# A routed expert kernel: first slot's products in float32, and token numbers with the one-hot as moving operand

## The chip, the cores and the metric

One core of a Trainium2 chip runs one kernel. The metric is the device time of one launch in microseconds (us), from the first to the last thing the core does. The engines are TensorE (PE, with PEld for its weight loads), VectorE (DVE), ScalarE (ACT), GpSimd (POOL) and SyncE (SP), which here only issues transfers. Each engine works through its own queue in order; semaphores hold an instruction until what it reads is there.

## What is computed

The reference has three stages. Attention with a memory term (4 batches, 8 heads, 576 positions, 64 wide) gives 2304 rows of 512. A router then assigns rows to 8 experts by a global greedy rule, 288 rows each, and expert e gives `relu(x[mask] @ w1[e]) @ w2[e]` (512 to 1024 to 512). Last, one dense layer for all rows: `h = x @ w_in`, `g = h * clip(h + 3, 0, 6) / 6`, `out = g @ w_out` (512 to 2048 to 512).

```python
for idx in order:                       # argsort(-logits.flatten())
    tok, e = int(idx) // E, int(idx) % E
    if assigned[tok] >= 0 or counts[e] >= cap:
        continue
    assigned[tok] = e
    counts[e] += 1
...
h = np.maximum(x[mask] @ w1[e], 0.0)
out[mask] = h @ w2[e]
```

All data are float32, and the assignment is discrete, so a product has to keep nearly all of float32's accuracy.

## The kernel before, in words

Attention fills the first 300 us and writes the rows to DRAM (`x_dram`). While it runs, `Convert` (L951) rounds part of w_in and w_out and puts them into DRAM as `wb`. Then `experts` (L1013) works in eight slots. A slot is one expert with its 288 tokens and has 24 chunks: 8 of the first kind (w1, w2 of that expert, 128 hidden units each) and 16 of the second (w_in, w_out). The list `order` (L1216) names them as (slot, kind, f), and one loop (L1261) goes through it.

A chunk has a first layer, `l1` (L1182), an evaluation `ev` (relu, or the clipped product), and a second layer, `l2` (L1212), which adds into four PSUM tiles `acc`. The second layer runs LAG = 2 chunks behind the first (`second`, L1231, with the list `pend`). Between the kinds `y_in` (L1173) copies the four sums to SBUF as the next kind's input; after the second kind `out_units` (L1143) transposes and scatters the result by token number.

Accuracy comes from splitting: a float32 value is written as hi + lo in float32r, and a product is three float32r products (hi with hi, hi with lo, lo with hi), so 12 for `l1` and 12 for `l2` of a chunk. For weights `split_w` (L1092) does it: ScalarE copies the raw tile to hi (L1106), GpSimd subtracts to get lo (L1108); in slot 0 the first six and then every sixth of these go to VectorE. `ahead` (L1221) calls it some chunks before their use. For the second kind the splits of odd chunks stay in SBUF (`WB`), those of even chunks go to DRAM (`hl`, L1112) and are loaded again in later slots (L1102). So slot 0 alone splits w_in and w_out. For activations the evaluation writes gh on ScalarE and gl on VectorE (L1201, L1208), and `x_in` and `y_in` do the same for x and y.

Raw weights come in through a ring of RAW = 4 tiles of 128x1024 (`load`, L1066), on SP's queue. The load of chunk f + 4 is issued when `split_w` has taken the second half of chunk f. In slot 0 the loads reach over both kinds; the last w_in/w_out pieces are rounded there (`Convert.rest`, L1004).

The router (`Router`, L515) finds each slot's expert and tokens while the slot before runs: `phase` (L804) searches two thresholds in four steps each on VectorE and ScalarE (L714, L716), `ids_units` (L916) turns positions into token numbers, and `gather` (L1056) fetches the rows with three indirect transfers on GpSimd's queue. For slot 0 nothing runs beside it. For the numbers, `oc` is a one-hot tile [128, 96, 20] (bfloat16), where `oc[:, :, j]` has a stride of 20 elements, and `ua` holds each token's number as 64 u + v, three times cumulated. The 20 products (L939, recorded on L701) have `oc[:, :, j]` as stationary and 6 columns of `ua` as moving operand; VectorE then copies, subtracts neighbours and joins u and v (L942 to L946).

The order on each engine's queue is set by a scheduler that simulates the program when it is built: it goes by program order and by its own estimate of when an instruction is ready. `step` (L1256) hands out the router's units at a rate per chunk, 1.4 in slot 0 and 0.9 later, and `mm` (L699) ties each router product behind the last product of the slot. On the chip the queues are then fixed: a TensorE product of the router whose input is late stops the slot's products behind it.

Of the kernel before, what the change touches and what calls it, by code (L numbers as in the profile page):

```python
# [514 lines left out]
class Router:  # L515
# [17 lines left out]
    def consts(self):  # L533
# [89 lines left out]
        sv = t("sv", [96, 4, 2])  # L623
        nc.vector.memset(sv, 0.0)
# [291 lines left out]
    def ids_units(self, pos, done):  # L916
# [96 lines left out]
def experts(ctx, tc, rt, x_dram, cv, w1, w2, out, ident, cap, B, S):  # L1013
# [7 lines left out]
    EVERY, FIRST = 6, 6  # L1021
# [44 lines left out]
    def load(s, j):  # L1066

        if j >= FA + FB * (s == 0):
            return
        if j >= FA:  # L1070
            f = j - FA
            raw = raws[s, 1, f] = wp.tile([128, 1024], F32, name="raw", tag="raw", bufs=RAW)
            if f < cv.pre // 2:
                nc.sync.dma_start(raw, cv.wb[:, f])
            else:
                conv.extend([lambda u=u: cv.rest(raw[:, u * 512:(u + 1) * 512], 2 * f + u) for u in range(2)])
            return
        f = j
# [3 lines left out]
        raw = wp.tile([128, 1024], F32, name="raw", tag="raw", bufs=RAW)  # L1082
        nc.sync.dma_start(raw[:, :512].rearrange("p (k n) -> p k n", k=KC),
                          w1[bass.ds(e, 1), :, f * 128:(f + 1) * 128].rearrange("o (k p) n -> p (o k) n", p=128))
        nc.sync.dma_start(raw[:, 512:], w2[bass.ds(e, 1), f * 128:(f + 1) * 128, :].rearrange("o p n -> p (o n)"))
        raws[s, 0, f] = raw
# [3 lines left out]
    cnt = [0]  # L1090

    def split_w(i, part):  # L1092
# [6 lines left out]
        W[i, part] = hi, lo  # L1099
# [16 lines left out]
    def mm3(p, lhs, rhs, first, last):  # L1116
        (ah, al), (bh, bl) = lhs, rhs
        nc.tensor.matmul(p, ah, bh, start=first, stop=False)  # L1118
        nc.tensor.matmul(p, ah, bl, start=False, stop=False)  # L1119
        rt.behind = nc.tensor.matmul(p, al, bh, start=False, stop=last)  # L1120

# [3 lines left out]
    def x_in(s):  # L1125

        XT[s] = []
        for c in range(KC):
# [6 lines left out]
            t = p[:, :cap]  # L1135
            if s:
                t = act.tile([128, cap], F32, name="t", tag="t", bufs=2)
                nc.scalar.activation(t, p[:, :cap], AF.Copy)
            rt.xin = nc.scalar.activation(hl[0], p[:, :cap], AF.Copy)
# [33 lines left out]
    def y_in(acc):  # L1173
        y = []
        for o, p in enumerate(acc):
            hl = parts("y", f"y{o}", 1)
# [3 lines left out]
        return y  # L1180

# [37 lines left out]
    nw = [0, 0]  # L1219

    def ahead(i):  # L1221

        for part in range(2):
            while nw[part] < min(i + 2 * SPLIT[0], len(order)):
                held = [j for j in range(i - part * LAG, nw[part] + 1) if j >= 0 and not (order[j][1] and order[j][2] % 2)]
                if len(held) > SPLIT[part] or order[nw[part]][0] not in reg or order[nw[part]][:1] + (0, 0) not in raws:
# [4 lines left out]
    def second():  # L1231
# [5 lines left out]
        l2(acc[s, kind], g, W.pop((i, 1)), f == 0, f == n - 1)  # L1237
        if f == n - 1:
            a = acc.pop((s, kind))
            if kind == 0:  # L1240
                X[s, 1] = y_in(a)
# [6 lines left out]
    for f in range(RAW):  # L1248
        load(0, f)
# [11 lines left out]
    for i, (s, kind, f) in enumerate(order):  # L1261
        step()
        if (kind, f) == (1, NEXT[s > 0]) and s + 1 < E:
            routed(s + 1)
            for u in range(RAW):
                load(s + 1, u)
# [12 lines left out]
        e = l1(kind, f, X[s, 1] if kind else XT[s], W.pop((i, 0)), rt.behind if kind and f == 1 else None)  # L1279
# [3 lines left out]
        pend.append((i, e()))  # L1283
        if (kind, f) in STORE and todo:
# [81 lines left out]
```

## Time and profile before

| | us |
|---|---|
| median of 3 runs | 1131.04 (1130.54 to 1137.7) |
| profiled execution, its own time | 1130.45 |
| its span, first to last instruction | 1128.6 |
| TensorE busy | 961.0 |
| VectorE busy | 727.9 |
| ScalarE busy | 605.6 |
| GpSimd busy | 435.8 |
[...]

Busy time is the union of an engine's instructions. Products on TensorE overlap in its pipeline, so the duration of one is longer than its share of the time: what counts is the distance between starts. Line numbers are those of the kernel before; router products all carry line L701. "idle before" in a row names what ended the idle time.

### The profile page before, as it was taken

The page shows a single profiled execution, that of the slowest core. Times are in us where ns is not written, and L with a number is a line of the kernel's source. Part 1 is how long each engine was busy: PE and PEld are TensorE (multiplying, and loading weights), DVE is VectorE, ACT ScalarE, POOL GpSimd, SP SyncE. Part 2 cuts the span into 40 slices and gives each one's busy share as a digit, 9 for nine tenths or more (in the row PEclk, how much of TensorE's full clock was granted, in tenths as well). Part 3 has the DMA queues.
Part 4 walks back from the last instruction along what each step waited for, and adds up shares of the span by engine and source line. Part 5 has one row for each costly group of instructions (what it writes and reads, how often), then busy time and mean ns, then how long its engine had stood idle before and what let it go on. Part 6 is the DMA issues. An engine that isn't in the chain of part 4 may idle for free.

```text
span 1128.6 us, 20123 instructions
## 1 busy us (share of the span) xinstructions
PE 961.0 (85%) x6748; PEld 885.6 (78%) x6748; DVE 727.9 (64%) x1933; ACT 605.6 (54%) x1499; POOL 435.8 (39%) x346
## 2 busy tenths in 40 slices
PE   4888888898317788789889889899989999999997
PEld 3676766675217688779789788889978999999996
DVE  7888897986773996783973856586385534234332
ACT  5786776875334764534653563455256235445442
POOL 7657556661424664331250044026104402603400
PEclk9999999998657997889999999899899899999999
DMA  7889879887133865349229525823752562572540
GB/s 172 240 239 258 232 205 266 206 228 202 43 99 112 297 214 163 96 146 270 84 73 286 138 75 195 222 82 119 232 148 68 183 202 90 182 243 73 181 159 21
DMA packets 122999, 190.28 MB, mean 169 GB/s; under 512 B 21904, under 2 KB 72464, under 8 KB 122896
## 3 DMA queue, kind: packets, MB, share of 16 engines
q1 hardware_dynamic: 119136, 179.54, 53.2%
q0 software_dynamic: 3072, 9.44, 2.8%
q8 instruction: 54, 0.88, 0.3%
q14 instruction: 49, 0.40, 0.1%
q10 hardware_dynamic: 688, 0.02, 0.0%
HBM read 144.60 MB, written 25.61 MB: 151 GB/s over the span
## 4 chain that ended last, share of the span: by engine, by line
PE 34%; DVE 20%; issue 8%; DMA 5%; ACT 1%; POOL 1%; POOLq 0%; DVEq 0%; ACTq 0%; SPq 0%
DVE rcmp L714 5%; PE h L1187 5%; PE acc L1119 5%; PE h L1188 5%; PE acc L1120 5%; PE h L1190 5%; PE acc L1118 5%; DMA rHw<-kd 4%; PE rp L701 2%; DVE gl L1201 2%; DVE gl L1208 2%; DVE cnt L717 1%; DVE t L1206 1%; DVE fl L725 1%; POOL w L1108 1%
## 5 line engine op out<-in xcount | busy, mean ns | idle before, releaser
L1108 POOL TENSOR_TENSOR w<-raw,w 128x512 fp32r<-128x512 f32 x135 | 180.6, 1352 | 383.5 <-ACT w L1106 291.4
L1119 PE MATMUL acc<-gl,w 128*128 128x288 f32 x512 | 156.7, 312 | 19.3 <-DVE gl L1208 13.0
L1120 PE MATMUL acc<-gh,w 128*128 128x288 f32 x512 | 153.4, 306 | 0.0
L1118 PE MATMUL acc<-gh,w 128*128 128x288 f32 x512 | 139.9, 310 | 13.7 <-ACT gh L1207 13.5
L1206 DVE SCALAR_TENSOR_TENSOR t<-t,pc 128x288 f32<-128x288 f32 x128 | 61.4, 480 | 117.4 <-ACT pc L1205 117.2
L1119 PEld LDWEIGHTS acc<-gl,w 128*128 128x128 f32 x512 | 101.8, 199 | 24.3 <-DVE gl L1208 16.7
L1204 ACT ACTIVATE t<-h,rthree 128x288 f32<-128x288 f32 x128 | 63.5, 496 | 102.8 <-PE h L1190 97.5
L1118 PEld LDWEIGHTS acc<-gh,w 128*128 128x128 f32 x512 | 93.9, 197 | 16.3 <-ACT gh L1207 16.2
L1106 ACT ACTIVATE w<-raw 128x512 fp32r<-128x512 f32 x144 | 89.6, 633 | 28.5 <-PE acc L1120 16.3
L282 ACT ACTIVATE P<-P,mx 128x128 f32<-128x128 f32 (+2 forms) x144 | 83.6, 581 | 37.1 <-DVE mx L267 35.7
L1120 PEld LDWEIGHTS acc<-gh,w 128*128 128x128 f32 x512 | 101.8, 199 | 0.0
L1201 DVE TENSOR_TENSOR gl<-t,gh 128x288 fp32r<-128x288 f32 x64 | 52.7, 824 | 73.6 <-ACT gh L1200 73.6
L1207 ACT ACTIVATE gh<-t 128x288 fp32r<-128x288 f32 x128 | 56.6, 444 | 64.4 <-DVE t L1206 64.4
L1208 DVE SCALAR_TENSOR_TENSOR gl<-t,gh 128x288 fp32r<-128x288 f32 x128 | 66.1, 517 | 29.8 <-ACT gh L1207 28.0
L1187 PE MATMUL h<-yh,w 128*128 128x288 f32 x256 | 74.4, 309 | 6.6 <-ACT pc L1205 6.6
L1119 PE MATMUL acc<-gl,WB 128*128 128x288 f32 x256 | 75.9, 303 | 2.7 <-DVE gl L1208 2.6
L246 PE MATMUL sc<-kh,qs 128*128 128x128 f32 (+3 forms) x128 | 49.7, 399 | 30.9 <-DVE qs L218 12.2
L1187 PE MATMUL h<-xh,w 128*128 128x288 f32 x256 | 75.3, 313 | 0.3 <-ACT gh L1200 0.3
L1120 PE MATMUL acc<-gh,WB 128*128 128x288 f32 x256 | 74.8, 298 | 0.0
L1188 PE MATMUL h<-xh,w 128*128 128x288 f32 x256 | 74.4, 310 | 0.0
L1188 PE MATMUL h<-yh,w 128*128 128x288 f32 x256 | 72.5, 301 | 0.0
L1187 PE MATMUL h<-yh,WB 128*128 128x288 f32 x256 | 71.1, 298 | 0.0
(294 smaller groups left out, 2806.8 us busy)
## 6 DMA issues: line engine op xcount, KB each, us to landing
w<-hl SPq DMA_DIRECT2D x112, 512.0 KB, 5.0
raw<-in_moe_w_dram SPq DMA_DIRECT2D x128, 256.0 KB, 4.3
kh<-knh SPq DMA_DIRECT2D x60, 144.0 KB, 2.6
raw<-in_moe_w_in_dram SPq DMA_DIRECT2D x16, 512.0 KB, 4.0
raw<-in_moe_w_out_dram SPq DMA_DIRECT2D x16, 512.0 KB, 4.6
hl<-w SPq DMA_DIRECT2D x16, 512.0 KB, 6.2
wb<-wf SPq DMA_DIRECT2D x28, 256.0 KB, 2.9
raw<-wb SPq DMA_DIRECT2D x14, 512.0 KB, 5.0
```

Source lines behind the costliest of these rows:

```text
L282: nc.scalar.activation(x[:, :w], x[:, :w], AF.Exp, bias=mx, scale=-1.0, accum_out=col)
L1106: nc.scalar.activation(hi, src, AF.Copy)
L1108: j = (nc.vector if v else nc.gpsimd).tensor_tensor(lo, src, hi.bitcast(F32), op=OP.subtract)
L1118: nc.tensor.matmul(p, ah, bh, start=first, stop=False)
L1119: nc.tensor.matmul(p, ah, bl, start=False, stop=False)
L1120: rt.behind = nc.tensor.matmul(p, al, bh, start=False, stop=last)
L1187: nc.tensor.matmul(p, wk[k][0], x[k][0], start=(k == 0), stop=False)
L1188: nc.tensor.matmul(p, wk[k][1], x[k][0], start=False, stop=False)
L1201: nc.vector.tensor_tensor(gl, t, gh.bitcast(F32), op=OP.subtract)
L1204: nc.scalar.activation(t, p, AF.Relu, bias=rt.three)
L1206: nc.vector.scalar_tensor_tensor(t, t, 6.0, pc, op0=OP.min, op1=OP.mult)
L1208: nc.vector.scalar_tensor_tensor(gl, t, 1.0 / 6.0, gh.bitcast(F32), op0=OP.mult, op1=OP.subtract)
```

## The change

Slot 0 uses float32 products on unsplit weights and activations: `l1_whole` for the first layer (4 products), one product for each of the four sums in `l2`, plain copies in `x_in` and `y_in` (odd ones on VectorE, even ones on ScalarE), one tile g instead of gh and gl. `ahead` starts with slot 1. The weights of the second kind are still split in slot 0, for later slots, but after the chunk's first layer and evaluation, and always on ScalarE and GpSimd. The ring has two tiles of 128x512 a chunk instead of one of 128x1024, and `load(i + RAW)` comes at the end of chunk i in slot 0; the first loads of slot 1 come out of the same sequence instead of with the expert's number. In the router, `ua` becomes the stationary operand and `oc[:, :, j]` the moving one; the result [6, 96] is copied to bfloat16 and turned by one product with a constant [6, 3] that subtracts neighbours and joins 64 u + v. Ten small VectorE instructions build that constant at the start.

```diff
@@ consts
-        sv = t("sv", [96, 4, 2])
-        nc.vector.memset(sv, 0.0)
+        dg = t("dg", [128, 3], BF)
+        nc.vector.tensor_scalar(ti[:, :1], pi, 1, None, op0=OP.logical_shift_right)
+        nc.vector.tensor_copy(bf, ti[:, :1])
+        nc.vector.tensor_scalar(ti[:, :1], pi, 1, None, op0=OP.bitwise_and)
+        nc.vector.tensor_copy(ef, ti[:, :1])
+        nc.vector.tensor_scalar(ef, ef, -63.0, 64.0, op0=OP.mult, op1=OP.add)
+        nc.vector.tensor_scalar(kb[:, 0:3], col[:, 0:3], bf, ef, op0=OP.is_equal, op1=OP.mult)
+        nc.vector.tensor_scalar(bf, bf, -1.0, None, op0=OP.add)
+        nc.vector.tensor_scalar(q2, col[:, 0:2], bf, ef, op0=OP.is_equal, op1=OP.mult)
+        nc.vector.tensor_tensor(kb[:, 0:2], kb[:, 0:2], q2, op=OP.subtract)
+        nc.vector.tensor_copy(dg, kb[:, 0:3])
@@ ids_units
-                self.mm(p[:96, :6], self.oc[:, :, j], st["ua"][:, j].rearrange("p a u -> p (a u)"),
+                self.mm(p[:6, :96], st["ua"][:, j].rearrange("p a u -> p (a u)"), self.oc[:, :, j],
                         start=(j == 0), stop=(j == NJ - 1))
-            sv = self.sv
-            nc.vector.tensor_copy(sv[:, :3], p[:96, :6].rearrange("p (a u) -> p a u", u=2))
-            d = wk.tile([96, 3, 2], F32, name="d", bufs=1)
-            nc.vector.tensor_tensor(d, sv[:, :3], sv[:, 1:], op=OP.subtract)
+            sv = wk.tile([6, 96], BF, name="sv", bufs=1)
+            nc.vector.tensor_copy(sv, p[:6, :96])
+            p = self.ps.tile([128, 512], F32, name="rp", tag="r", bufs=2)
+            self.mm(p[:96, :3], sv, self.dg[:6], start=True, stop=True)
             ids = wk.tile([96, 3], I32, name="ids", bufs=2)
-            self.last = nc.vector.scalar_tensor_tensor(ids, d[:, :, 0], 64.0, d[:, :, 1], op0=OP.mult, op1=OP.add)
+            self.last = nc.vector.tensor_copy(ids, p[:96, :3])
@@ load
-    def load(s, j):
+    def load(j):
+        s, kind, f = order[j]
+        if s and kind:
             return
...
+        raw = raws[j] = [wp.tile([128, 512], F32, name=f"raw{u}", tag=f"raw{u}", bufs=RAW) for u in range(2)]
+        if kind:
+            for u in range(2):
+                if f < cv.pre // 2:
+                    nc.sync.dma_start(raw[u], cv.wb[:, f, u * 512:(u + 1) * 512])
+                else:
+                    conv.append(lambda u=u: cv.rest(raw[u], 2 * f + u))
             return
...
@@ split_w
-        src = raws[s, kind, f][:, part * 512:(part + 1) * 512]
-        cnt[0] += 1
+        src = raws[i][part]
         nc.scalar.activation(hi, src, AF.Copy)
-        v = s == 0 and (cnt[0] % EVERY == 0 or cnt[0] <= FIRST)
-        j = (nc.vector if v else nc.gpsimd).tensor_tensor(lo, src, hi.bitcast(F32), op=OP.subtract)
-        if s == 0 and kind == 0:
-            after(tc, j, rt.last if v else rt.fetch)
+        nc.gpsimd.tensor_tensor(lo, src, hi.bitcast(F32), op=OP.subtract)
         if kind and f % 2 == 0:
             nc.sync.dma_start(hl[f // 2, part], w.bitcast(F32))
-        if part:
-            load(s, f + kind * FA + RAW)
+        if part and s and f + RAW < FA:
+            load(i + RAW)
@@ x_in (y_in alike)
+            if s == 0:
+                x = whole("x", f"x{c}", 1)
+                if c % 2:
+                    nc.vector.tensor_copy(x, p[:, :cap])
+                else:
+                    nc.scalar.activation(x, p[:, :cap], AF.Copy)
+                XT[s].append(x)
+                continue
@@ new
+    def l1_whole(kind, f, x, w, prev=None):
+        p = ps.tile([128, 512], F32, name="h", tag="h", bufs=2)[:, :cap]
+        for k in range(KC):
+            rt.behind = nc.tensor.matmul(p, w[:, k * 128:(k + 1) * 128], x[k], start=(k == 0), stop=(k == KC - 1))
...
+        def ev():
+            g = whole("g", "g", LAG + 2)
+            if kind == 0:
+                nc.scalar.activation(g, p, AF.Relu)
+            else:
...
+                nc.scalar.activation(t, p, AF.Relu, bias=rt.three)
+                nc.scalar.activation(pc, p, AF.Copy, scale=1.0 / 6.0)
+                nc.vector.scalar_tensor_tensor(g, t, 6.0, pc, op0=OP.min, op1=OP.mult)
+            return g
+        return ev
@@ l2
+            if not isinstance(g, tuple):
+                rt.behind = nc.tensor.matmul(p[:, :cap], w[:, o * 128:(o + 1) * 128], g, start=first, stop=last)
+                continue
@@ ahead
-    nw = [0, 0]
+    nw = [FA + FB] * 2
@@ main loop
-            for u in range(RAW):
-                load(s + 1, u)
+            for u in range(RAW if s else 0):
+                load(pos[s + 1, 0, u])
...
         pend.append((i, e()))
+        if s == 0:
+            for u in range(2 * kind):
+                split_w(i, u)
+            load(i + RAW)
```

## Rows read from the trace of the kernel before

**Rows 1.** First line of the page
```profile
span 1128.6 us, 20123 instructions
```

**Rows 2.** Stretches: length; busy (count) of PE, PEld, DVE, ACT, POOL; clock; DMA share, GB/s
```profile
346.70:466.20 119.50, 97.78 (x630) 91.75 (x630) 92.17 (x191) 72.37 (x163) 63.03 (x47) 0.87 0.59 192
466.20:567.80 101.60, 91.32 (x635) 87.13 (x633) 75.90 (x204) 52.76 (x126) 28.96 (x22) 0.95 0.46 145
959.30:1038.60 79.30, 78.94 (x602) 78.68 (x601) 28.22 (x53) 39.16 (x97) 26.92 (x22) 1.00 0.53 174
346.70:350.00 3.30, 3.30 (x14) 3.30 (x15) 2.67 (x7) 0.85 (x3) 0.00 (x0) 0.52 0.00 0
```

**Rows 3.** Waits of TensorE in slot 0: us in total, times, longest
```profile
PE acc L1118 <- ACT gh L1207: 6.2, 3, 4.3
PE acc L1119 <- DVE gl L1208: 5.1, 5, 1.9
PE rp L701 <- DVE roc L933: 3.8, 1, 3.8
```

**Rows 4.** Groups by line, VectorE, slot 0
```profile
L1208 DVE SCALAR_TENSOR_TENSOR gl<-t,gh 128x288 fp32r<-128x288 f32 x15 | 8.8, 589 | 1.0 <-ACT gh L1207 1.0
L1201 DVE TENSOR_TENSOR gl<-t,gh 128x288 fp32r<-128x288 f32 x8 | 6.5, 808 | 9.1 <-ACT gh L1200 9.1
```

**Rows 5.** Timeline of TensorE, attention: start us, us, then the merged instructions
```profile
127.65 1.84 PE L328 MATMUL av<-PT,vn 128*64 128x320 f32 x12
128.24 0.44 PE L328 MATMUL av<-PT,vn 128*64 128x320 f32 x2
128.51 0.71 PE L328 MATMUL av<-PT,vn 128*64 128x320 f32 x4
```

**Rows 6.** The same view, slot 6's first kind
```profile
959.30:987.60 28.30, 28.30 (x218) 28.28 (x217) 8.18 (x15) 13.60 (x33) 16.96 (x14) 1.00 0.56 182
```

**Rows 7.** Router's products (L701) by stretch (PE, PEld), one group, a hand-over
```profile
327.90:331.40 3.50, 3.46 (x20) 3.46 (x20) 0.50 0.88 284
892.45:895.80 3.35, 3.31 (x20) 3.35 (x20) 1.00 0.92 319
L701 PE MATMUL rw<-rXT,rR 128*128 128x512 bf16 (+1 forms) x16 | 3.5, 292 | 0.0
325.54 0.16 DVE L895 TENSOR_SCALAR ex<-rp 128x2 f32<-128x2 f32 x1 [0.31 <-PE rp L701]
```

**Rows 8.** Around slot 0's gather: timelines of POOL, DVE, SP; landing
```profile
332.41 4.95 POOL L1061 DMA_INDIRECT xg<-x_dram,ids  x1 [23.49 <-DVE rleft L914]
338.89 0.92 POOL L1061 DMA_INDIRECT xg<-x_dram,ids  x1 [0.30 <-issue]
333.84 2.48 DVE L1108 TENSOR_TENSOR w<-raw,w 128x512 fp32r<-128x512 f32 x4
335.24 0.38 SPq L1083 DMA_DIRECT2D raw<-in_moe_w_dram  x1
xg<-x_dram,ids POOLq DMA_INDIRECT x3, 6.8
xg<-x_dram,ids POOLq DMA_INDIRECT x3, 5.1
```

**Rows 9.** SP's timeline; transfers of slot 0 with landing; splits on the page
```profile
420.98 0.55 SPq L1083 DMA_DIRECT2D raw<-in_moe_w_dram  x1
raw<-wb SPq DMA_DIRECT2D x14, 512.0 KB, 5.0
raw<-in_moe_w_dram SPq DMA_DIRECT2D x16, 256.0 KB, 9.5
L1106 ACT ACTIVATE w<-raw 128x512 fp32r<-128x512 f32 x144 | 89.6, 633 | 28.5 <-PE acc L1120 16.3
L1108 POOL TENSOR_TENSOR w<-raw,w 128x512 fp32r<-128x512 f32 x135 | 180.6, 1352 | 383.5 <-ACT w L1106 291.4
```

**Rows 10.** Timeline of TensorE, its first product
```profile
12.02 0.48 PE L246 MATMUL sc<-kh,qs 128*128 128x128 f32 x1 [12.02 <-DVE qs L218]
```

More of the change, by code (lines that the diff above doesn't have):

```diff
@@ L1081, in load @@
         e = reg[s]
-        raw = wp.tile([128, 1024], F32, name="raw", tag="raw", bufs=RAW)
-        nc.sync.dma_start(raw[:, :512].rearrange("p (k n) -> p k n", k=KC),
+        nc.sync.dma_start(raw[0].rearrange("p (k n) -> p k n", k=KC),
                           w1[bass.ds(e, 1), :, f * 128:(f + 1) * 128].rearrange("o (k p) n -> p (o k) n", p=128))
-        nc.sync.dma_start(raw[:, 512:], w2[bass.ds(e, 1), f * 128:(f + 1) * 128, :].rearrange("o p n -> p (o n)"))
-        raws[s, 0, f] = raw
+        nc.sync.dma_start(raw[1], w2[bass.ds(e, 1), f * 128:(f + 1) * 128, :].rearrange("o p n -> p (o n)"))
     W = {}
     conv = []
-    cnt = [0]
     def split_w(i, part):
@@ L1098, in split_w @@
         hi, lo = w[:, :512], w[:, 512:]
-        W[i, part] = hi, lo
+        if s:
+            W[i, part] = hi, lo
         if kind and s:
@@ L1120, in mm3, with whole @@
         rt.behind = nc.tensor.matmul(p, al, bh, start=False, stop=last)
+    def whole(name, tag, bufs):
+        return act.tile([128, cap], F32, name=name, tag=tag + "h", bufs=bufs)
     def parts(name, tag, bufs):
@@ L1133, in x_in @@
                 nc.tensor.transpose(p[:, a * G:(a + 1) * G], XG[s][a][:, c * 128:(c + 1) * 128], ident[:G, :G])
-            hl = parts("x", f"x{c}", 1)
[L1135 to L1139, printed above, removed]
+            if s == 0:
[6 more added lines that the diff above has]
+                continue
+            hl = parts("x", f"x{c}", 1)
+            t = act.tile([128, cap], F32, name="t", tag="t", bufs=2)
+            nc.scalar.activation(t, p[:, :cap], AF.Copy)
+            nc.scalar.activation(hl[0], p[:, :cap], AF.Copy)
             nc.vector.tensor_tensor(hl[1], t, hl[0].bitcast(F32), op=OP.subtract)
@@ L1180, in y_in @@
         return y
+    def l1_whole(kind, f, x, w, prev=None):
+        p = ps.tile([128, 512], F32, name="h", tag="h", bufs=2)[:, :cap]
+        for k in range(KC):
+            rt.behind = nc.tensor.matmul(p, w[:, k * 128:(k + 1) * 128], x[k], start=(k == 0), stop=(k == KC - 1))
+            if prev is not None:
+                after(tc, rt.behind, prev)
+                prev = None
+        def ev():
+            g = whole("g", "g", LAG + 2)
+            if kind == 0:
+                nc.scalar.activation(g, p, AF.Relu)
+            else:
+                t = act.tile([128, cap], F32, name="t", tag="t", bufs=2)
+                pc = act.tile([128, cap], F32, name="pc", tag="pc", bufs=2)
+                nc.scalar.activation(t, p, AF.Relu, bias=rt.three)
[3 more added lines that the diff above has]
+        return ev
     def l1(kind, f, x, w, prev=None):
@@ L1224, in ahead @@
             while nw[part] < min(i + 2 * SPLIT[0], len(order)):
-                held = [j for j in range(i - part * LAG, nw[part] + 1) if j >= 0 and not (order[j][1] and order[j][2] % 2)]
-                if len(held) > SPLIT[part] or order[nw[part]][0] not in reg or order[nw[part]][:1] + (0, 0) not in raws:
+                held = [j for j in range(max(i - part * LAG, FA + FB), nw[part] + 1)
+                        if not (order[j][1] and order[j][2] % 2)]
+                if len(held) > SPLIT[part] or nw[part] not in raws and not order[nw[part]][1]:
                     break
@@ L1236, in second @@
             acc[s, kind] = [ps.tile([128, 512], F32, name=f"acc{o}", tag=f"acc{o}") for o in range(KC)]
-        l2(acc[s, kind], g, W.pop((i, 1)), f == 0, f == n - 1)
+        l2(acc[s, kind], g, W.pop((i, 1)) if s else raws[i][1], f == 0, f == n - 1)
         if f == n - 1:
@@ L1240, in second @@
             if kind == 0:
-                X[s, 1] = y_in(a)
+                X[s, 1] = y_in(s, a)
             else:
@@ L1248, in experts @@
     for f in range(RAW):
-        load(0, f)
+        load(f)
     for i in range(2):
@@ L1278, in experts @@
             conv.pop(0)()
-        e = l1(kind, f, X[s, 1] if kind else XT[s], W.pop((i, 0)), rt.behind if kind and f == 1 else None)
+        e = (l1 if s else l1_whole)(kind, f, X[s, 1] if kind else XT[s], W.pop((i, 0)) if s else raws[i][0],
+                                    rt.behind if kind and f == 1 else None)
         step()
```

17 lines of the change are left out of this document (6 added, 11 removed).

## The prediction, made before the result was known

> **What bounds the kernel now.** I read the span first, then busy time by stretch, then the waits of TensorE in the one stretch that the change rewrites. The profiled execution spans 1128.6 us [rows 1]; its own time is 1130.45, so 1.85 lies around the span, and it stands 0.6 below the median of the three runs (1131.04). All sums below are made against 1130.45. The eight slots begin at 346.7 us. Slot 0 takes 119.5 us to slot 1's first product, slot 1 101.6, and slot 6 79.3 with TensorE busy for 78.9 at a granted clock of 1.00 [rows 2]. So late slots are bound by TensorE alone, and slot 0 loses 40 us. [...] The waits name what it starves on: the two halves of g (6.2 + 5.1 us) and the one-hot positions (3.8 us) [rows 3]; all six waits of that list come to 21.7 us. The g halves cost VectorE 8.8 + 6.5 us, at 589 and 808 ns each [rows 4], and each chunk has to wait for its own.
>
> **Part 1, float32 products in slot 0.** Removed before the products: all splits of w1 and w2 (16 halves), the hi/lo work on x, y and g. The 32 splits of w_in and w_out stay, but come after the chunk's products and nobody in slot 0 waits for them. Each group of three float32r products becomes one float32 product: per chunk 8 in place of 24. The price of one: in attention six float32 products of 320 columns (three blocks, two heads) leave 12 records, so two records each [rows 5]. Records of the two heads run side by side (the pair at 128.24 takes 0.44 us together), and the next pair starts at 128.51: a step of 0.27 us; over all six pairs it is (1.84 - 0.44) / 5 = 0.28. That is 0.84 ns a column and record, so 288 columns cost 0.243 us a record, 0.486 a product. A float32r product goes by at 28.3 us / 218 = 0.130 us [rows 6], weight load included, so 128-column loads fit under 0.243. A chunk is then 8 x 0.486 = 3.89 us in place of 24 x 0.130 = 3.12. TensorE alone gets slower by 0.77 x 24 = 18 us over the slot; what is bought is the idle time.
>
> Slot 0's stretch holds 24 first and 22 second layers (two are late, beside slot 1): 46 x 4 x 0.486 = 89.4 us. To it: the start at the lower clock, 3.3 us at 0.52 [rows 2], which loses 1.6; the router's and transposes' work on TensorE, 3.5 + 3.5 us in rows [rows 7] and some 1.5 of small ones, 8.5; and waits that stay, 5 us (the one-hot 3.8 as now, 1 where y is copied). The g waits go: two chunks of lag are now 7.8 us, against the 0.6 us of the one VectorE step that an evaluation keeps, and what is queued before it. Sum 104.5, gain 15.0. Bounds: 19 with no wait left; 8 if the router's in-order stops grow to the 10 to 12 us that fit slot 1 (101.6 - 79.3 less its router work). The two late second layers cost 2 x (1.94 - 1.56) = 0.7 in slot 1.
>
> **Start of slot 0.** Now the gather is slow: its first issue holds GpSimd 4.95 us against 0.92 for the third, while VectorE runs four more weight splits of 0.68 us (2.48 together), and from 335.24 on three more chunks are loaded (split early, they freed the ring), in front of the last gathered rows, which take 6.8 us to land; slot 1's take 5.1 [rows 8]. After the change those VectorE splits are gone, and the ring lets chunk 4 load only after the first product, so both obstacles go. Landing: 332.4 + two issues of 1.2 (0.92 and the step between) + 5.1 gives 340 in place of 338.9 + 6.8 = 345.7; if the 4.95 is a first issue's own cost, 338.9 + 5.1 = 344. Gain 2 to 6; I take 4.5, nearer to the first, as the splits beside the slow issue are what differs, less a little for the transposes, which then come in one lot.
> [...]
>
> **Start of slot 1: what is late next.** Slot 1's first chunks are now loaded from 421 us on [rows 9], 45 us ahead. After the change they pass through the same ring of four: the second half of chunk i is freed by products two chunks on, and SP's queue is in order, so the next chunk's first half, the intermediate stores and the router's transfers all stand behind it. The lead is two chunks, 7.8 us in slot 0, about 7.0 at the seam. Inside slot 0 it needs 0.8 for two issues and 5.0 to land: it holds. At the seam a split follows, 0.63 on ScalarE and 1.35 on GpSimd [rows 9]: 0.8 + 5.0 + 2.0 = 7.8, over by 0.8; with the 9.5 us that these 256 KB loads took in this stretch, 12.3. Each chunk pays half the excess, about five do: 2 to 11 us, zero if the loads go early. I take 4.
>
> **Part 2, token numbers.** The 20 products of one slot fill some 3.4 us, 0.17 each, at a granted clock of 0.50 (3.46 us) and of 1.00 (3.31) alike [rows 7]. They are 6 columns long, so the load of the 96-column weight, read with a stride of 20 elements, sets the pace, and no clock. After the change the same 96 strided columns stream as moving operand. No row shows a strided moving operand. Upper bound: the same 0.17 (nearest row, the same tile and stride): no gain. Lower bound: 0.130 / 288 x 96 = 0.043 us each, 0.9 us in all, 2.5 less a slot. I take the nearest row. The turn adds a copy, a product and a copy for copy, subtract, multiply: one hand-over through TensorE and back, 0.31 us [rows 7], against two VectorE steps of 0.2; the products behind it on TensorE wait if nothing of the slot is set between. +0.5 over eight slots.
> [...]
>
> **Constants.** Ten small VectorE instructions replace one memset, ahead of the first queries' split, on which TensorE's first product waits until 12.02 [rows 10]: at 0.1 us each +1.0 (0 to 1.3).
>
> **Sum.** -15.0 + 0.7 - 4.5 + 4.0 + 0.5 + 1.0 = -13.3: 1130.45 - 13.3 = 1117.
>
> **Rivals.** (a) The moving form is fast: up to 2.5 us in each of eight slots, where it lies on TensorE's queue; 20 at most, 12 likely, so 1105. For: the queue stands still during every one of these groups. Against: the pace ignores the clock, as a memory limit would. (b) The gain is given back at the seam and in the router's stops: 11 us at the loads and 10 of waits in slot 0 leave 1129 at worst, 1126 as its centre; slot 1 shows such stops now, 101.6 us against slot 6's 79.3 [rows 2]. (c) Slower: the ring of four becomes the bound of slot 0. If a load takes L to land, a chunk cannot be shorter than (L + 0.8) / 2. At 5.0 it sleeps; from 7.0 it stretches the chunk; at the 9.5 of [rows 9] a chunk is 5.15 and 20 chunks lose 25 us: 1142. It makes the kernel slower than before from L = 8.3 on. For: loads and stores of the second kind then ask 1 MB a chunk, some 270 GB/s, where the stretch now moves 192 [rows 2]. Against: float32 chunks are slow enough to give each load 7.8 us, and 9.5 was measured on loads that were queued far ahead. (d) Float32 is not the price I read, because attention's are 64 weights wide: full price at 128 would be up to twice as much only if the pair did not share the array, and the paired starts say that it does; 0.02, within (c).
>
> **How the numbers follow.** Forecast 0.42, (a) 0.28, (b) 0.20, (c) 0.10. About 1% is what a measurement of this kernel can tell from no change, so the bounds are 1119.7 and 1142.4. Faster: 0.7 of the forecast's spread (1108 to 1125) and nearly all of (a), 0.57; within: the rest and (b), 0.34; slower 0.09. The range leaves out the far end of (a) and most of (c): 1098 to 1132; the forecast's own is 1108 to 1125.
>
> **What would show it.** Right: slot 0 near 105 us to slot 1's first product, clock near 1.00 after its start, float32 records 0.24 us apart; the first product near 341; a stop at slot 1's first splits behind loads; token products still 0.17 us apart. Wrong: second-kind chunks over 4.5 us with TensorE waiting for raw loads (c); token products under 0.1 us apart (a); slots 1 to 4 longer than now by more than the seam (b).

## The result, and the profile after

The changed kernel takes 1142.78 us (median of 20 runs, 1133.52 to 1152.68), the kernel before 1133.16 (20 runs beside them): ratio 1.009, 95% interval 1.0067 to 1.0113. It is slower by some 10 us, where 13 us faster was forecast, and it lies outside the range of 1098 to 1132. The profiled execution took 1142.45.

First line of the page of the changed kernel:

```profile
span 1140.7 us, 19718 instructions
```

Its stretches, columns as in [rows 2]: slot 0, slot 1, slot 6; then the token products of slot 0 and of slot 6; then two stretches of 5 us inside slot 0.

```profile
343.90:475.80 131.90, 112.80 (x438) 82.67 (x438) 87.13 (x177) 60.29 (x129) 54.03 (x41) 0.90 0.56 180
475.80:581.10 105.30, 94.36 (x630) 88.65 (x631) 72.19 (x179) 52.13 (x124) 32.08 (x26) 0.92 0.50 150
970.90:1050.60 79.70, 79.11 (x602) 78.86 (x601) 28.51 (x53) 39.23 (x97) 26.91 (x22) 1.00 0.55 174
331.90:335.55 3.65, 3.60 (x20) 1.98 (x20) 0.55 (x1) 0.00 (x0) 0.00 (x0) 0.50 0.92 290
903.05:906.70 3.65, 3.65 (x22) 2.06 (x21) 0.00 (x0) 0.00 (x0) 0.00 (x0) 0.90 0.92 308
385.50:390.50 5.00, 5.00 (x11) 3.57 (x12) 4.83 (x11) 2.37 (x5) 2.32 (x2) 0.50 0.14 20
390.50:395.50 5.00, 5.00 (x22) 3.95 (x21) 4.86 (x13) 3.63 (x8) 2.07 (x2) 1.00 0.67 220
```

Read the first column of figures against the second: slot 0 is 131.9 us long with TensorE busy for 112.8, so it idles 19.1; before it was 119.5, 97.8 and 21.7 [rows 2]. The idle time that was to be bought is nearly all still there, and the busy time grew by 15. The last two lines show why busy time alone says little: at a granted clock of 0.50, half of full speed as the profile counts it, five microseconds hold 11 records of float32, at 1.00 they hold 22. The 20 token products of slot 0 fill 3.60 us; before they filled 3.58, of which the stretch in [rows 7], cut off at 331.40, holds 3.46.

What TensorE waits for in slot 0 (us in total, times, longest):

```profile
PE acc L1256 <- DVE g L1219: 4.6, 2, 2.5
PE xt L1140 <- ACT pc L1218: 3.6, 1, 3.6
PE h L1205 <- POOL raw L998: 3.5, 1, 3.5
PE h L1228 <- ACT xh L1152: 2.6, 1, 2.6
PE h L1205 <- DVE y L1192: 2.6, 1, 2.6
PE h L1205 <- ACT y L1194: 2.1, 1, 2.1
```

The waits for gh and gl of [rows 3] are gone by name; g, pc, y, the rounding (`raw`, L998) and slot 1's first xh stand in their place, 19 us where the forecast left 5. The two waits for y stand where the second kind begins, before the search for slot 2's threshold. What held pc and g back is that search. ScalarE's timeline (idle time and its cause in brackets) has, at the head of the queue, the search's first count, waiting for its keys, and the t and pc of a chunk behind it; VectorE stands there too, for 6.72 us:

```profile
445.37 1.01 ACT L726 ACTIVATE rcmp<-rHw,rT 128x864 bf16<-128x864 uint16 x1 [7.53 <-DMA rHw<-kd]
446.29 0.19 ACT L726 ACTIVATION_READ_ACCUMULATOR rcmp<-rHw,rT 128x1 f32 x1
446.38 0.48 ACT L1217 ACTIVATE t<-h,rthree 128x288 f32<-128x288 f32 x1
446.76 0.40 ACT L1218 ACTIVATE pc<-h 128x288 f32<-128x288 f32 x1
```

The start of slot 0 did get shorter. GpSimd's gather issues, where [rows 8] had 4.95 for the first, and their landing:

```profile
336.60 1.33 POOL L1070 DMA_INDIRECT xg<-x_dram,ids  x1 [23.70 <-DVE rleft L924]
339.47 1.08 POOL L1070 DMA_INDIRECT xg<-x_dram,ids  x1 [0.30 <-issue]
...
xg<-x_dram,ids POOLq DMA_INDIRECT x3, 3.4
```

From the first token product to the slot's first product there are 12.0 us, before 18.8.

### The profile page after: what moved, and what is told of

Read it like the earlier page. It is cut to its first block, busy times and chain, and to the rows that moved or that the text cites. A ratio compares the mean times of both kernels' runs of the same rounds, so it can differ in the third digit from the quotient of the medians.

```text
span 1140.7 us, 19718 instructions
## 1 busy us (share of the span) xinstructions
PE 984.0 (86%) x6564; PEld 871.4 (76%) x6564; DVE 715.8 (63%) x1893; ACT 587.8 (52%) x1455; POOL 423.6 (37%) x343
## 4 chain that ended last, share of the span: by engine, by line
PE 43%; DVE 27%; issue 12%; DMA 11%; ACT 3%; POOL 2%; SPq 1%; POOLq 0%; DVEq 0%; ACTq 0%
DVE rcmp L724 6%; PE acc L1122 5%; PE h L1228 5%; PE h L1229 4%; PE acc L1123 4%; PE h L1231 4%; PE acc L1121 4%; DMA rHw<-kd 4%; PE h L1205 3%; PE rp L711 2%; PE av L328 2%; PE acc L1256 2%; DVE fl L735 2%; DVE P L267 1%; DMA raw<-in_moe_w_out_dram 1%
## 5 line engine op out<-in xcount | busy, mean ns | idle before, releaser
L1113 POOL TENSOR_TENSOR w<-raw,w 128x512 fp32r<-128x512 f32 x128 | 169.4, 1339 | 382.5 <-ACT w L1112 267.4
L1122 PE MATMUL acc<-gl,w 128*128 128x288 f32 x448 | 135.6, 308 | 12.6 <-DVE gl L1249 8.0
L1121 PE MATMUL acc<-gh,w 128*128 128x288 f32 x448 | 125.3, 308 | 10.4 <-ACT gh L1248 9.2
L1123 PE MATMUL acc<-gh,w 128*128 128x288 f32 x448 | 134.0, 304 | 0.0
L1122 PEld LDWEIGHTS acc<-gl,w 128*128 128x128 f32 x448 | 87.8, 196 | 16.0 <-DVE gl L1249 10.7
L1121 PEld LDWEIGHTS acc<-gh,w 128*128 128x128 f32 x448 | 82.6, 195 | 12.8 <-ACT gh L1248 11.3
L1123 PEld LDWEIGHTS acc<-gh,w 128*128 128x128 f32 x448 | 88.0, 196 | 0.4 <-issue 0.3
L1242 DVE TENSOR_TENSOR gl<-t,gh 128x288 fp32r<-128x288 f32 x56 | 41.3, 737 | 69.7 <-ACT gh L1241 69.7
L246 PE MATMUL sc<-kh,qs 128*128 128x128 f32 (+3 forms) x128 | 50.0, 402 | 32.4 <-DVE mx L267 16.9
L1228 PE MATMUL h<-xh,w 128*128 128x288 f32 x224 | 66.3, 313 | 2.6 <-ACT xh L1152 2.6
L1240 ACT ACTIVATE t<-h 128x288 f32<-128x288 f32 x56 | 23.0, 412 | 88.2 <-PE h L1231 77.1
L1228 PE MATMUL h<-yh,w 128*128 128x288 f32 x224 | 63.8, 303 | 4.6 <-ACT pc L1246 4.6
L1229 PE MATMUL h<-xh,w 128*128 128x288 f32 x224 | 65.6, 312 | 0.0
L267 DVE CUSTOM_DVE_ANT_0 P<-sc,mask 128x128 f32<-128x128 f32 (+3 forms) x128 | 59.3, 479 | 9.9 <-PE sc L247 4.0
```

Source lines behind the costliest of these rows:

```text
L267: nc.vector.tensor_tensor_reduce(out=x[:, c0:c0 + cw], in0=sc[:, :cw], in1=m, scale=-scale, scalar=init, op0=OP.add, op1=OP.min, accum_out=mx)
L1113: nc.gpsimd.tensor_tensor(lo, src, hi.bitcast(F32), op=OP.subtract)
L1228: nc.tensor.matmul(p, wk[k][0], x[k][0], start=(k == 0), stop=False)
L1229: nc.tensor.matmul(p, wk[k][1], x[k][0], start=False, stop=False)
```

## The experiments

My first theory from these two traces (T): float32 does what was forecast, and the loss is the rounding of the last weight pieces at the end of slot 0.

**The two parts apart, and the rounding left out.** `ids_only` is the kernel before with the new token numbers; `f32_only` is the changed kernel with the old ones. In `after_norest` and `before_norest` the last four pieces are not loaded and rounded in slot 0; two pairs that lie rounded in DRAM are read in their place (the lines are of `after_norest`; `before_norest` does the same with its whole tiles):

```diff
-                if f < cv.pre // 2:
-                    nc.sync.dma_start(raw[u], cv.wb[:, f, u * 512:(u + 1) * 512])
-                else:
-                    conv.append(lambda u=u: cv.rest(raw[u], 2 * f + u))
+                nc.sync.dma_start(raw[u], cv.wb[:, f % 14, u * 512:(u + 1) * 512])
...
-    for i in range(2):
-        cv.load(cv.pre + i)
```

> The kernel before with the new token numbers alone (constants dg, products with the one-hot as moving operand, turn product); its slot 0 stays in two float32r parts. The trace of the changed kernel shows the gather 6.8 us shorter, but the attention stretch 4.0 us longer (token numbers begin at 331.9 instead of 327.9). Theory T (the loss of the whole change lies at the end of slot 0 in the late rounding): this half is a small gain, 1127 to 1131 us if the 4.0 us come from the new constants (ratio 0.994 to 0.998), 1126 if they were another execution's accident (0.993); slot 0 stays at 119 to 120 us. Rival S (the constants at the start cost more than the gather gains): 1134 to 1140, ratio above 1.001.

> The changed kernel with the old token numbers: float32 in slot 0, with its ring of pieces, alone. Theory T: slot 0 still takes 130 to 133 us instead of 119.5, the gather again 15 us, the attention's end again at 328: 1144 to 1149 us, ratio 1.010 to 1.015. Rival S (constants are the loss): 1130 to 1138, below 1.004, with the slot 0 no longer than 125 us.

> The changed kernel without the rounding inside slot 0: the last two pairs of rounded pieces are read from the rounded pieces 0 and 1 of the store in DRAM, so the rounding of four pieces (and their loads) is left out. Theory T (the late rounding, behind the router's search on VectorE, stops slot 0's last chunks): slot 0 falls from 131.8 to 105 to 112 us, total 1116 to 1124 us, ratio 0.985 to 0.992. Rival R (the search's own wait for the transfer of the keys stops TensorE, rounding or not): slot 0 stays above 125 us, total 1136 or more. Rival P (float32 products and the boundary between the kinds are the loss): slot 0 stays above 122 us with the stretch up to 443 unchanged at 99 us; total 1133 or more.

> The kernel before without the rounding inside slot 0 (the same edit: the last two pairs read from pieces 0 and 1). Theory T: here the rounding is early and lies beside TensorE's work, so taking it away gives 0 to 4 us: 1129 to 1133, slot 0 115 to 119.5 us. If the rounding costs as much here as in the changed kernel (15 us or more), total 1118 or less, then its place in the changed kernel is not the cause of the loss.

Measured: `ids_only` 1.0111 (1.0064 to 1.0159), `f32_only` 1.0031 (0.9998 to 1.0064), `after_norest` 1.0078 (1.0047 to 1.0108), `before_norest` 0.9938 (0.9908 to 0.9967). All four speak against T. The token numbers, which I had held for a small gain, are the larger loss; float32 alone is no gain and hardly a loss; the rounding costs 7 us in the kernel before and next to nothing in the changed one, whose slot 0 still takes 129.0 us without it. Rival S, a loss ahead of slot 0, is not seen in its place: in `ids_only` the token numbers begin at 328.5 us, in the kernel before at 327.9. Slots 0 and 1 of `f32_only`:

```profile
342.10:465.80 123.70, 109.59 (x437) 82.44 (x437) 83.57 (x191) 61.37 (x131) 54.48 (x41) 0.92 0.60 184
465.80:575.50 109.70, 94.85 (x629) 90.39 (x630) 69.17 (x167) 51.49 (x122) 31.54 (x26) 0.92 0.52 153
```

Some of slot 0's idle time did go here (14.1 us are left of 21.7), but slot 1's grew from 10.3 to 14.9: there TensorE waits 6.0 us for ScalarE's gh (0.4 before).

**Where the token numbers cost.** `before_again` is the kernel before once more, for its scatter from one execution to the next. `ids_slot0` takes the new form for slot 0 alone:

```diff
-        return [u0, u2]
+        return [u0, u2_old if s else u2]
```

> The kernel before, unchanged, for a second profile of it. If its executions scatter by place as the token numbers' start did (327.7 to 331.9 us over six profiles, whichever constants), slot 0 stays within 4 us of 119.5 and slot 1 comes nearer to the 105 to 110 us of the other kernels than to 101.6; ratio 0.996 to 1.004. If slot 1 is 101 to 103 us again, the 105 to 110 of the variants are theirs.

> The kernel before with the new token numbers for slot 0 alone, where TensorE has nothing else to do; the other seven slots take them in the old way, the new constants stay. Theory J (the turn product puts a second trip from TensorE to VectorE and back into slots that are running, which sets the gather and the next routing about 4 us later): the loss of the full new token numbers (ratio 1.011) goes, ratio 0.995 to 1.002, 1129 to 1137 us. Rival S (the new constants, or anything ahead of slot 0): the loss stays, 1.008 to 1.014.

Measured: `before_again` 1.001 (0.9983 to 1.0038), `ids_slot0` 0.9992 (0.9962 to 1.0021). So theory J's place holds: the loss is in slots that are running, and the new constants, which `ids_slot0` has too, are not it: rival S had 1.008 or more. Slots 0 and 1 of `before_again`:

```profile
352.40:474.10 121.70, 98.47 (x629) 92.18 (x630) 93.05 (x191) 72.13 (x163) 61.54 (x47) 0.86 0.59 189
474.10:577.40 103.30, 92.47 (x635) 88.51 (x634) 76.24 (x204) 53.24 (x126) 28.93 (x22) 0.94 0.49 146
```

and of `ids_only`:

```profile
344.40:467.10 122.70, 97.52 (x631) 89.00 (x631) 93.54 (x191) 72.69 (x164) 61.85 (x47) 0.89 0.59 187
467.10:577.20 110.10, 93.79 (x635) 86.92 (x634) 79.00 (x203) 53.28 (x127) 27.80 (x22) 0.94 0.46 137
```

The 110 us of slot 1 are the variant's own. Its timeline on VectorE shows the step that is new, the copy to sv and then, 4.41 us later, the token numbers; in between TensorE runs slot products, which the scheduler had put ahead of the turn:

```profile
439.86 0.24 DVE L951 CAST sv<-rp 6x96 bf16<-6x96 f32 x1 [0.45 <-PE rp L710]
...
444.27 0.16 DVE L955 CAST ids<-rp 96x3 int32<-96x3 f32 x1 [0.33 <-PE rp L710]
```

Three kernels ask what in this costs. `ids_first` ties the next slot product behind the turn (the same in `l1`); `old_trip` keeps the old products and adds only a second trip; `ids_bank` writes the turn into the tile that is there (its lines are against `ids_only`; the names behind # are not in the kernels):

```diff
+        pin(nc.tensor.matmul(p, ah, bh, start=first, stop=False))   # ids_first: after(tc, i, rt.turned)
...
+            nc.vector.tensor_copy(svb, p[:96, :6])                  # old_trip
+            p = self.ps.tile([128, 512], F32, name="rp", tag="r", bufs=2)
+            self.mm(p[:96, :6], self.idb[:96, :96], svb, start=True, stop=True)
...
-            p = self.ps.tile([128, 512], F32, name="rp", tag="r", bufs=2)
+            self.mm(p[:96, 256:259], sv, self.dg[:6], start=True, stop=True)   # ids_bank
```

> The kernel before with the new token numbers in all slots, and the first product of a slot that is written after the turn product made to come behind it, so that the turn stands right behind the twenty token products on TensorE instead of some 20 to 40 slot products later. TensorE then waits for VectorE's copy, 0.25 us plus the passes between the engines, some 0.6 us seven times. Theory J (the late turn sets the gather and the next routing's transposes 4 us later, which stops the end of slot 0 and slot 1): slot 1's token numbers come within 1 us of their products again, slot 0 and slot 1 fall from 122.7 and 110.2 to 119 to 121 and 102 to 105 us, ratio 0.998 to 1.005 instead of 1.011. Rival (the round trip itself is dear wherever it stands): ratio 1.008 or more.

> The kernel before with its old token products, and behind them one more product with a small identity (exact, so the numbers stay the same) between two copies of VectorE: the second trip from TensorE to VectorE and back without the new form of the products. SyncE's and GpSimd's orders become those of the kernel with the new token numbers alone. Theory J' (the trip, and the order of the queues that comes with it, is the whole cost of the new token numbers): ratio 1.008 to 1.014, slot 0 at 122 to 124 us and slot 1 at 107 to 111. Rival M (the one-hot as moving operand costs something that the pace of 0.171 us does not show): ratio 0.997 to 1.003, slot 1 at 101 to 104.

> The kernel before with the new token numbers in all slots, the turn product written into free columns of the PSUM tile that the token products fill, so that no second tile of that ring of two is taken for it. If it is the ring of two tiles that holds the next routing's transposes back (they share its tag), slot 1 falls from 110.2 to 102 to 105 us and the ratio from 1.011 to 0.999 to 1.005. If it is the trip (theory J'), the transposes of the next routing still stand behind the turn on TensorE and the ratio stays at 1.008 to 1.014.

Measured: `ids_first` 1.0161 (1.0114 to 1.0208), a miss: the turn stands at once behind the products, TensorE waits only 0.34 us for it, and yet slot 0 is 129.7 us long. A late turn is thus not the cause by itself; holding the slot's products behind it made TensorE wait 6.3 us for the one-hot (3.8 before). `old_trip` 1.0087 (1.0056 to 1.0117), with slots of 122.3 and 111.3 us: the trip alone, with the old products, costs what the new token numbers cost. `ids_bank` 1.0048 (1.002 to 1.0076): by the medians about half of it goes when the turn takes no second tile of the ring that it shares with the next routing, but the intervals of the three overlap, so this half is likely and not shown. Slots 0 and 1 of `old_trip`:

```profile
346.00:468.30 122.30, 97.25 (x630) 90.50 (x631) 94.72 (x193) 72.57 (x164) 62.35 (x47) 0.89 0.58 188
468.30:579.60 111.30, 96.22 (x636) 91.95 (x636) 79.56 (x205) 53.20 (x127) 27.97 (x22) 0.91 0.45 135
```

Two of TensorE's waits in it, the first in slot 0, the second in slot 1:

```profile
PE xt L1137 <- ACT xh L1143: 6.1, 2, 4.9
PE acc L1122 <- ACT gh L1211: 5.3, 4, 2.1
```

The first is a transpose of the gathered rows that waits for ScalarE's xh. It is there in `ids_only` (5.9) and in `ids_bank` (5.6) too, and not in the kernel before or in `ids_slot0`; the second is 0.4 before. So what the trip adds to TensorE's waits is work of ScalarE that comes later than before.

**What keeps TensorE waiting in the float32 slot.** Theory K: the search for slot 2. `f32_late` (old token numbers) and `after_late` (new ones) hold the router still from slot 1's token numbers until slot 1 runs; `f32_lag3` (old ones) gives g one chunk more, and loads the ring's second half a chunk later for it:

```diff
-        hold[0] -= RATE[s > 0]
+        hold[0] -= RATE[s > 0] if s or 1 not in IDS else 0
...
-        if len(pend) == LAG:
+        while len(pend) >= LAG + (s == 0):      # f32_lag3
```

> Float32 in slot 0 with the old token numbers, and the router's units held from the token numbers of slot 1 until slot 1 runs, so that the search for slot 2 (eight counting steps) leaves the last 35 us of slot 0 and lies in slot 1. Theory K (slot 0's last chunks wait for ScalarE and VectorE, whose queues stand at the search and its transfer): slot 0 falls from 123.7 to 108 to 114 us, slot 1 grows by 0 to 8 us, total 1124 to 1132 us, ratio 0.990 to 0.998. Rival P (the float32 products, the stop between the kinds and the half clock behind it are the loss): slot 0 stays above 119 us, ratio 1.002 or more.

> The changed kernel with the same edit: no unit of the router between the token numbers of slot 1 and the start of slot 1. Theory K: slot 0 falls from 131.8 to 110 to 117 us, slot 1 grows by 0 to 8 us, ratio 0.994 to 1.003 instead of 1.009; what stays above the run with the old token numbers is the turn product's. Rival P: slot 0 above 125 us, ratio 1.007 or more.

> Float32 in slot 0 with the old token numbers, and in slot 0 the second layer three chunks behind the first instead of two (the ring's second half is loaded one chunk later for it), so that a late g has about 3.9 us more before TensorE needs it. The search for slot 2 stays in slot 0. Theory K (slot 0's last chunks wait for VectorE's g and ScalarE's t and pc behind the search's steps): the waits for g go (7 us in the run with two chunks), slot 0 falls from 123.7 to 113 to 119 us, total ratio 0.993 to 0.999 instead of 1.003. Rival R2 (the work of the queues is the bound, not the time between a result and its use): the waits move to the two PSUM buffers of the first layer, slot 0 stays above 121 us, ratio 1.000 to 1.006.

Measured: `f32_late` 1.0071 (1.0036 to 1.0106), `after_late` 1.0094 (1.0058 to 1.0129), `f32_lag3` 1.0024 (0.9987 to 1.0061). Slots 0 and 1 of `after_late`:

```profile
341.90:453.60 111.70, 104.28 (x434) 77.76 (x435) 62.35 (x134) 53.62 (x115) 52.81 (x40) 0.96 0.59 188
453.60:578.40 124.80, 99.80 (x632) 91.45 (x633) 70.22 (x180) 55.34 (x128) 32.57 (x28) 0.88 0.51 149
```

and of `f32_late`:

```profile
340.90:453.90 113.00, 106.34 (x434) 81.46 (x435) 66.11 (x135) 53.46 (x114) 51.49 (x41) 0.93 0.58 186
453.90:578.00 124.10, 100.29 (x630) 93.08 (x631) 70.44 (x181) 55.02 (x127) 32.37 (x27) 0.86 0.50 150
```

K is right on slot 0: without the search it falls by 20.2 us (10.7 in `f32_late`) and idles 7.4 us, near the 5 that I had forecast for all of it. What is left is mostly y, the second kind's input, in `f32_late`:

```profile
PE h L1196 <- ACT y L1185: 2.7, 1, 2.7
PE h L1196 <- DVE y L1183: 2.5, 1, 2.5
```

The 0 to 8 us expected of slot 1, and the ratios below 1.003, are wrong: slot 1 grows by 19.5 and 14.4. Moved there, the router's work stops TensorE in slot 1. A longer lag only moves the waits, now to the rounding and to the first layer's two tiles; slot 0 became 134.4 us. TensorE's waits in slot 0 of `f32_lag3`:

```profile
PE h L1201 <- POOL raw L989: 6.0, 1, 6.0
PE acc L1252 <- DVE g L1215: 5.9, 4, 2.9
PE h L1201 <- ACT y L1190: 4.6, 1, 4.6
PE h L1201 <- ACT pc L1214: 3.1, 2, 2.2
```

**The rounding moved into the attention.** Both kernels: `PRE = 32`, `PACE = 4, 3`, no rounding in slot 0.

> The kernel before with all 32 pieces rounded during the attention (a rounding after every 4th item instead of every 5th), none in slot 0. Without the rounding in slot 0 its time was 0.9938 of the kernel before. If the attention hides four more pieces: ratio 0.993 to 0.997. If they lie on the attention's path at their own price (VectorE's four operations of some 2 us a piece in all, four times, and the earlier rhythm): 0.999 to 1.006.

> Float32 in slot 0 with the old token numbers, all 32 pieces rounded during the attention. Theory K (search and rounding share the queues at the end of slot 0): slot 0 falls from 123.7 to 114 to 121 us and slot 1 from 109.7 to 104 to 108 us, ratio 0.993 to 1.001 if the attention hides the four pieces. Rival R2 (the queues' search alone is the bound, as the changed kernel without rounding, at 1.0078, says): slot 0 stays above 121 us, ratio 1.001 to 1.007.

Measured: 1.0056 (1.0025 to 1.0088) and 1.0148 (1.0105 to 1.0191). The attention does not hide the four pieces: token numbers begin at 343.0 and 341.4 us. Slot 0 is 115.5 in the first and 125.8 in the second (123.7 in `f32_only`), so the float32 slot does not become shorter when the rounding leaves it.

**Two versions that are faster.** `before_pool6` leaves the kernel before as it is but for the six subtractions at the start of slot 0; `hybrid` keeps float32 for the first kind of slot 0 alone (`l1 if i >= FA else l1_whole`, splits from chunk FA on, old token numbers).

```diff
-        v = s == 0 and (cnt[0] % EVERY == 0 or cnt[0] <= FIRST)
+        v = s == 0 and cnt[0] % EVERY == 0 and cnt[0] > FIRST
```

> The kernel before, but the first six subtractions of slot 0 (the lower parts of its first pieces) on GpSimd behind its three gathers instead of on VectorE. In the traces GpSimd's first gather issue takes 4.95 us wherever these six run on VectorE beside it (four profiles), and 1.33 us in the float32 kernels, which have none. Theory G (the shorter start of slot 0 comes from these six operations and not from the token numbers): first issue 1.3 us, from the token numbers' first product to the slot's first product 12 to 15 us instead of 18.8, ratio 0.994 to 0.998 if GpSimd's six subtractions (1.35 us each) come in time for the first chunks. Against it: 18 us or more, or the first kind of slot 0 longer by as much as the start is shorter; ratio 0.999 or more.

> Float32 in the first kind of slot 0 alone (eight chunks), two parts as in the kernel before in its second kind, old token numbers. Theory K: the short start of slot 0 stays (11.8 us instead of 18.8), the first kind is 3 to 4 us longer than with parts (37.1 against 33.4 us), the second kind, in which the search lies, takes 84 to 88 us as before, and slot 1 comes back to 101 to 105 us; ratio 0.995 to 0.999. Rival: the ring in two halves or the splitting itself spoils the second kind; slot 0 above 124 us or slot 1 above 106, ratio 1.002 or more.

Measured: `before_pool6` 0.990 (0.9859 to 0.994), `hybrid` 0.9944 (0.9917 to 0.9972); medians 1121.71 and 1128.39 us beside 1135.05. GpSimd's timeline in `before_pool6`:

```profile
328.23 1.34 POOL L1061 DMA_INDIRECT xg<-x_dram,ids  x1 [23.50 <-DVE rleft L914]
...
332.21 8.66 POOL L1108 TENSOR_TENSOR w<-raw,w 128x512 fp32r<-128x512 f32 x7
```

The first issue is down from 4.95 to 1.34 us, and the slot begins 11.8 us after the first token product instead of 18.8, with the old products, and slot 0 is not longer for it (114.4): theory G holds. The gain of 11 us by the ratio is more than these 7. In the profiled execution 4.2 more lie ahead of the token numbers (323.76 us against 327.94) and 2.1 in slots 0 and 1, both no more than two executions of one kernel differ by; where the rest of the ratio lies was not tried. Slot 0 of `hybrid`, its first kind, its second kind:

```profile
340.50:458.30 117.80, 99.65 (x559) 88.05 (x561) 88.98 (x187) 65.13 (x145) 54.94 (x40) 0.88 0.67 208
340.50:376.00 35.50, 34.63 (x144) 26.13 (x145) 16.04 (x35) 16.84 (x36) 6.50 (x5) 0.96 0.45 140
376.00:458.30 82.30, 65.02 (x416) 61.92 (x417) 72.95 (x153) 48.29 (x109) 48.43 (x36) 0.84 0.77 237
```

Its slot 1 takes 108.2 us, a miss: 101 to 105 were expected, and above 106 was the rival's sign. Slots 0 and 1 together are not shorter than before (226.0 against 221.1 and 225.0). Its gain is seen at the start of slot 0, 11.8 us instead of 18.8, and `before_pool6` has that without a float32 product.

## Why the prediction was wrong, step by step

One table carries it. It adds slots 0 and 1 of each profile; idle is length less TensorE's busy time, from the rows above or the same view of the other runs. Each row is one execution, and the two of the kernel before differ by 3.9 us, so smaller differences say nothing.

| kernel | length | busy | idle |
|---|---|---|---|
| before, `before_again` | 221.1, 225.0 | 189.1, 190.9 | 32.0, 34.1 |
| `f32_only` | 233.4 | 204.4 | 29.0 |
| `f32_late`, `f32_lag3` | 237.1, 237.2 | 206.6, 205.9 | 30.5, 31.3 |
| `after_norest`, `f32_pre32` | 234.5, 232.1 | 204.5, 201.2 | 30.0, 30.9 |
| changed kernel, `after_late` | 237.2, 236.5 | 207.2, 204.1 | 30.0, 32.4 |
| `ids_slot0` | 222.6 | 190.8 | 31.8 |
| `ids_only`, `old_trip` | 232.8, 233.6 | 191.3, 193.5 | 41.5, 40.1 |
| `ids_bank`, `ids_first` | 230.3, 236.3 | 193.2, 195.0 | 37.1, 41.3 |
| `before_norest`, `before_pre32` | 216.9, 220.7 | 186.1, 193.4 | 30.8, 27.3 |
| `before_pool6`, `hybrid` | 219.0, 226.0 | 189.1, 194.5 | 29.9, 31.5 |

From profile to profile the changed kernel is 12.1 us longer: 4.0 ahead of the token numbers, where the kernel before scatters by more than that, -6.8 at the start of slot 0, 16.0 in slots 0 and 1, and -1.2 in the other six. Slot 0 itself missed its forecast of 104.5 by 27.4 us: 14.1 of them are idle time (19.1 against 5) and 13.3 busy time (112.8 against 99.5).

- **Float32 in slot 0 (forecast -15.0): the step that failed is "the g waits go".** The price of a product was right (records 0.24 us apart at a granted clock of 1.00; 18 us dearer over the slot by the forecast, 13 to 18 by the table). But the forecast paid for it with idle time, which was 119.5 less 97.8, and named the g halves as its cause. They were only the last to come in. VectorE and ScalarE also carry the search, whose count stands at the head of their queues, and without the halves TensorE waits for g, pc and the rounding behind the same steps. Over two slots the idle time is 29 to 32 us with float32 and 27 to 34 without it and without the trip; the higher price is paid, and hardly anything comes back. Shown by `f32_late`, `after_late` and `f32_lag3`: move the search or the lag, and the idle time moves along. Why the sum over both slots stays so nearly the same was not settled.
- **"Waits that stay, 5 us", mis-sized apart from the search.** The one-hot's 3.8 is gone from slot 0, but y, put at 1, is waited for 4.7 us, and 5.2 in `f32_late`, where slot 2's search is not in the slot.
- **"The start at the lower clock, 1.6", mis-sized.** In slot 0 of the changed kernel 42 of 376 float32 records stand about 0.47 us apart in five stretches, 19.8 us together, with a granted clock of 0.5 to 0.6; at 0.24 they would take 10.1. So the lower clock costs 9.7 us, because not only at the start but also behind stops of 2.2 to 3.6 us TensorE was granted 0.50 for some microseconds (11 records against 22 above). That is 8.1 of the 13.3 us of busy time. Another 1.9 is a misreading: the stretch holds 23 second layers, not 22, in the kernel before ([rows 2]'s slot 0 has 276 float32r products of them, 12 each) and in the changed one (376 records, 8 to a layer). The other 3.3 were not traced.
- **Start of slot 0 (-4.5): right, and larger.** 6.8 us here: 3.6 by the first issue, the rest by the last rows' landing (3.3 us; 5.1 was taken, 6.8 stood before). The first issue's excess went with the VectorE splits: 4.95 us in `before_again`, `ids_slot0` and `old_trip` as well, 1.34 in `before_pool6`, which has the first six on GpSimd. So it is not a first issue's own cost; how a split beside the issue holds it was not shown.
- **Start of slot 1 (+4.0).** Slot 1 grew by 3.7 us (101.6 to 105.3), but its first wait is 2.6 us for ScalarE's xh; no load was waited for at the seam. The size agrees by luck, the cause does not. (By the forecast's own lead of 7.0 us its upper bound would have been 13 and not 11, as slot 0's best gain would have been 20 and not 19; neither changes the sum.)
- **Token numbers (+0.5): the second failed step, "one hand-over through TensorE and back, 0.31 us against two VectorE steps of 0.2".** The pace was right: strided, the moving operand goes at 0.17 us a product as the weights did, at granted clocks of 0.50 and of 0.90, so rival (a) fell. What sets this pace was not shown: TensorE's weight loads were busy for 3.46 of 3.50 us in [rows 7] and are for 1.98 of 3.65 here. The trip was priced by its length. It costs 0.9 to 1.1% when nothing else is changed (`old_trip`, `ids_only`), as 6 to 9.5 us more of idle time in slots 0 and 1. A part is likely the ring tile (`ids_bank`). The rest may be the order of the queues that the scheduler makes with the trip in it; this was argued and not shown, and which change of the order costs was not settled. Beside float32 the two do not add up: 1.009 for both, 1.0031 for float32 alone and 1.0111 for the token numbers alone.
- **Constants (+1.0): not settled.** The 0.1 us for each was an estimate; in the kernel before VectorE's one-column steps at 6.2 us take 0.14 or 0.15 us and start 0.05 to 0.07 apart. `ids_slot0` has them and is at 0.9992, but its interval of some 3 us either way cannot tell 1 us. In the changed kernel's trace two of the ten run ahead of the first queries' split and TensorE's first product comes at 13.82 us, 1.8 later than in [rows 10]; in `ids_only` and `ids_slot0`, with the same ten, it comes at 11.52 and 12.05.
- **Rivals.** (b), the gain given back at the seam and in the router's stops, had a part of the mechanism and 0.20: it is the router that takes the gain back, but through VectorE's and ScalarE's queues and not through stops of its own products, and no load was waited for at the seam. Its centre of 1126 kept the search's stops where they were seen and lacked the trip. (c) had a time near the measured one, 1142, for a reason that did not occur: in slots 0 and 1 of all the kernels with float32 TensorE waited for a load of the ring once, 1.0 us in `f32_lag3`. That is luck.

## What to carry to other kernels

Before an idle time is counted as gain, ask what else stands in the queues of the engine that is named: the wait's name is the last one in, and where a fixed piece of work (here the search) passes through the same two engines, the idle time moves to the next name. A second trip between two in-order engines is priced by a run with the trip alone, not by its length. And two operations that meet by accident, here six subtractions beside a gather's issue, can be worth more than the rewriting around them.

## What the runs showed of the hardware that was not expected

What followed a stop was dear here: in the 5 us after the wait at the kinds' boundary TensorE was granted 0.50 and passed 11 float32 records, in the next 5 us 22. It is not float32 alone: in the kernel before float32r products came 0.24 us apart from 347.1 to 349.5 us, at 0.50, and 0.13 from 350.1 us on, at 1.00; in `ids_only` 0.24 apart from 440.6 us on and 0.13 from 442.5 on. The same program scatters ahead of its slots: token numbers began at 327.9 us in one profile of the kernel before and at 333.4 in the other, which is more than most terms of the forecast.

The first gather issue took 4.95 us in seven profiles with the six subtractions beside it, 1.33 or 1.34 in the nine without them, and 2.54 in two with them, `ids_only` and `before_pre32`. In these two VectorE's third subtraction starts 0.19 us after the second ends, in the seven 0.15 to 0.16; whether that lets the issue through was not tried.
